# A hand-ordered prologue rewritten: halved dense units, four rotating PSUM banks, and the tail keys first on SyncE's queue

## Chip, core and metric

The kernel runs on one core of a Trainium2 chip. The metric is the device time of one execution in microseconds; the number given for the kernel before is the median of 13 runs.

## The reference

Two stages. The first is chunked attention for 4 batches, 8 heads, 768 positions and head size 64; every chunk of 32 positions sees 16 positions to its left, 8 to its right, and 8 memory rows. The second is a gated feed-forward layer on the 3072 x 512 result:

```python
for c in range(nc):
    k_full = np.concatenate([mem_k, k[:, :, l_start:r_end]], axis=2)
    v_full = np.concatenate([mem_v, v[:, :, l_start:r_end]], axis=2)
    scores = scale * np.matmul(q_c, k_full.transpose(0, 1, 3, 2))
    a = softmax(scores)
    out[:, :, c_start:c_end] = np.matmul(a, v_full)
x = out.transpose(0, 2, 1, 3).reshape(B * S, H * D)
gate = np.maximum(x @ w_gate, 0.0)
val = x @ w_val
return gate * val @ w_out
```

The softmax is written here as a call; the reference computes it with maximum, exponential and sum. The weights are 512 x 1536, 512 x 1536 and 1536 x 512.

## The kernel before

**Blocks, steps and units.** The 3072 rows are cut into 8 blocks of 384 rows, two to a batch. In each block the attention is done in four steps of 96 queries (three chunks at once, against a band of 120 keys and 8 memory rows, with a mask for what a chunk may not see). A step has scores (TensorE, L251, with the mask added by two matmuls at L245 where the step masks there), an exponential (ScalarE, L258), a mask by product (VectorE, L265, where it doesn't), values (TensorE, L269, with the sum in an extra column), a division (VectorE, L275 and L278) and a transposition of the result into `xT`.

The dense layer of a block has 12 units of 128 hidden columns. A unit multiplies `xT` by a column block of the gate weights (four matmuls of 384 columns, L299), takes the relu (ScalarE, L304), does the same with the value weights, and multiplies both (VectorE, L310) into `gvT`. Three output tiles (L329, L338) follow when all 12 units are there.

**The ordered prologue.** From block 2 on, loops set the order: the attention of a block lies between the dense units of the one before, its K and Q are turned by DMA transposes (L186, L191). Ahead of that, blocks 0 and 1 are written out by hand in the string `ORDER`. Every token is one piece of work: `ck01:D` casts the second half of K of block 0 on VectorE (D is VectorE, A ScalarE, P GpSimd), `key2` makes the key bands of a pair of heads by matmuls with a shifted unit matrix (L361), `key2e:A` evacuates them, `q01` and `kt0` turn Q and K on TensorE, `S3`, `x3`, `M3`, `P3`, `n3`, `T3`, `e3` are the parts of step 3 (steps 0 to 3 are of block 0, 4 to 7 of block 1), `G2` gathers V for a step (L394), `fg01`, `fr01`, `fv01`, `fm01` are gate, relu, value and product of unit 1 of block 0, `d3` is a warm-up of three small matmuls, and `wa`, `wA`, `wb`, `wc` load growing pieces of the gate and value weights. Each engine runs its own instructions in the order in which the tokens come.

The first four units of blocks 0 and 1 stand in `ORDER`. The units 4 to 11 of these blocks follow from a list `units`, with a table `hook` of what is done after which unit: at unit 0 and 1 ScalarE casts block 2's K and SyncE turns it, at 4 and 5 the same for Q, and the scores of block 2 begin at unit 13.

**PSUM.** Eight banks: 0 and 1 for the scores of even steps, 2 and 3 for the values, 4 and up for everything that `bank()` hands out in rotation. In the prologue the scores of odd steps use banks 6 and 7 (`self.sb`), so the rotation has two banks (`NG = [2]`); after the exponential of step 7 it has four.

**Loads.** SyncE issues the list `LOADS` in order: K and Q of block 0 in halves (`lk01`, `lk00`, `lq00`, `lq01`), V's extra rows (`lvx`), K of block 1, V of block 0 in halves, Q of block 1, and V of block 1 step by step. The extra keys of block 0 (8 memory rows, 8 tail rows, tile `kx`) come over ScalarE's and GpSimd's queues. GpSimd issues the weights. Its first weight load waits for Q of block 1, by a copy of one element:

```python
GATE = raw["q"][0:1, 1, 0, 0, 0:1]
            if nm == "wa":
                pl(gate, GATE)
```

In the same way the loads of block 2 on SyncE's queue, and the last weight loads, wait for the third pair of weight loads (`wc`):

```python
pl(raw["k"][0:1, 0, 0, 0, 0:1], w_gate_sb[0:1, 0, 1023:1024])
load_kq(2)
load_w(1024, 512)
```

Of the kernel before, what the change touches and what calls it, by code (L numbers as in the profile page):

```python
# [8 lines left out]
F16 = mybir.dt.float16  # L9

ALU = mybir.AluOpType
# [4 lines left out]
def kernel(  # L16
# [14 lines left out]
    B, H, S, D = q.shape  # L31
# [3 lines left out]
    QB = 96  # L35
# [4 lines left out]
    MB = 384  # L40
    NJ = MB // QB
    NT = MB // 128
    NBLK = B * S // MB
    NFC = DM // 128
    NDC = DFF // 128
    VW = D + 2
    R3 = 3
# [7 lines left out]
    xpool = ctx.enter_context(tc.tile_pool(name="xpool", bufs=4))  # L55
    xtpool = ctx.enter_context(tc.tile_pool(name="xtpool", bufs=2))
    gvpool = ctx.enter_context(tc.tile_pool(name="gvpool", bufs=2))
    grpool = ctx.enter_context(tc.tile_pool(name="grpool", bufs=3))
    opool = ctx.enter_context(tc.tile_pool(name="opool", bufs=6))
    pspool = ctx.enter_context(tc.tile_pool(name="pspool", bufs=1, space=bass.MemoryType.PSUM))  # L60
    ctx.enter_context(tc.manual_schedule())
# [1 line left out]
    PS = pspool.tile([128, 8, 512], F32, name="PS")  # L63
    rot = [0]

    NG = [2]

    def bank():
        n = 4 + rot[0] % NG[0]
        rot[0] += 1  # L70
        return n

    dve, act, pool, pe, sp = nc.vector, nc.scalar, nc.gpsimd, nc.tensor, nc.sync
# [9 lines left out]
    kx = wpool.tile([2 * NMEM, 2, H, D], F32, name="kx")  # L83
    vx = wpool.tile([2 * NMEM, H, D], F32, name="vx")
    kx16 = wpool.tile([128, H, D], F16, name="kx16")
    vx16 = wpool.tile([128, H, D], F16, name="vx16")
# [9 lines left out]
    ke = wpool.tile([128, R3, HP, NMEM], F16, name="ke")  # L96
# [3 lines left out]
    w_gate_sb = wpool.tile([128, NFC, DFF], F16, name="w_gate_sb")  # L100
    w_val_sb = wpool.tile([128, NFC, DFF], F16, name="w_val_sb")
# [22 lines left out]
    def turned_mask(name, product):  # L124
        d = (masks if product else negp)[name] = wpool.tile([128, QB], F16, name=f"{'mask' if product else 'negp'}_{name}")
        o = d.rearrange("p (t c) -> p t c", t=R3)
        i = neg[name].rearrange("p (c t) -> p t c", t=R3)
        if product:
            pool.tensor_scalar(out=o, in0=i, scalar1=-1.0, scalar2=None, op0=ALU.is_ge)  # L129
        else:  # L130
            pl(o, i)
# [14 lines left out]
    def rows(t, b, tok, parts):  # L146
        return bass.AP(tensor=t.tensor, offset=t[b, 0, tok, 0].offset, ap=[[D, parts], [S * D, H], [1, D]])

    def kx_rows(eng, b, d, t, mem, eng2=None):
        eng.dma_start(d[0:NMEM], mem[b].rearrange("h n d -> n h d"))  # L150
        (eng2 or eng).dma_start(d[NMEM:2 * NMEM], rows(t, b, MB, NMEM))
# [17 lines left out]
    def cast3(eng, c, n, a0=0, na=HP):  # L169
        i = n % 2  # L170
        d = (kn[:, i, 0:R3].rearrange("p t a c -> p a t c") if c == "k" else qn[:, i])[:, a0:a0 + na]
        eng(d.rearrange("p a t (x d) -> p a x t d", x=2),  # L172
            raw[c][:, i, 2 * a0:2 * a0 + 2 * na].rearrange("p (a x) t d -> p a x t d", x=2))
# [119 lines left out]

    gvT, xTs = {}, {}

    def dff_mm(n, w_sb, m):
        o = PS[:, bank(), 0:MB]
        for f in range(NFC):
            pe.matmul(o, lhsT=w_sb[:, f, 128 * m:128 * m + 128], rhs=xTs[n][:, f], start=(f == 0), stop=(f == NFC - 1))  # L299
        return o  # L300

    def relu(g_ps):
        g_relu = grpool.tile([128, MB], F16, name="g_relu")
        act.activation(g_relu, g_ps, ACT.Relu)  # L304
        return g_relu

    def product(n, m, vl_ps, g_relu):
        if n not in gvT:
            gvT[n] = gvpool.tile([128, NDC, MB], F16, name="gvT")
        dve.tensor_tensor(out=gvT[n][:, m].rearrange("p (t j c) -> p t j c", t=R3, j=NJ),  # L310
                          in0=vl_ps.rearrange("p (j t c) -> p t j c", t=R3, j=NJ),
                          in1=g_relu.rearrange("p (j t c) -> p t j c", t=R3, j=NJ), op=ALU.mult)

    def dff(n, m, mid=()):
        g = relu(dff_mm(n, w_gate_sb, m))
# [69 lines left out]
    def cast_v3(eng, h0=0, nh=H):  # L385
        eng(v16[:, h0:h0 + nh], vlong[:, 0, h0:h0 + nh])
# [11 lines left out]

    dve.memset(warm, 0.0)
    act.activation(warm, warm, ACT.Exp)  # L400
    kx_rows(act, 0, kx[:, 0], k, mem_k, pool)
    LOADS = "lk01 lk00 lq00 lq01 lvx lk1 lv01 lv00 lq1 lvm lv10 lv13 lv11 lv12".split()
    for tok in LOADS:
        c, r = tok[1], [int(ch) for ch in tok if ch.isdigit()]
        if tok == "lvx":
# [15 lines left out]
    def keep(n):  # L421
        for _ in range(n):
            pe.matmul(PS[:, 3, 4 * VW:512], lhsT=zero[:, 0:128], rhs=zero[:, 0:512 - 4 * VW], start=True, stop=True)
# [32 lines left out]
    for n in EARLY:  # L456
# [3 lines left out]

    ac = act.copy
    GATE = raw["q"][0:1, 1, 0, 0, 0:1]
    keep(20)
    st = [Step(0, j) for j in range(NJ)] + [Step(1, j) for j in range(NJ)]
    ORDER = """
        kx16:D ck01:D key2 ck00:D key3 key2e:A d3 key0 cq01:P key0e:A key3e:D key1 d3 q01 ke key1e:A cq00:P kee:A
        q01e:D q00 q00e:D ck11:P ck10:A vx16:D cv00:D d10 kt1 cv01:P S0 kt0 kt0e:D S1 kt1e:A x0:A b0:D G0 M0:D S2
        x1:A g0:A G1 P0 x2:A g1:A M1 G2 bm:D mlast:P bi0:D bi2:P wa:P cq11:D cq10:A n0:D q11 P1 S3 g2:A cv10:A M2:D
        q11e:D q10 n1:D x3:A G3 P2 q10e:D g3:A wA:P S4 x4:A M3 n2:D bi1:D T0 P3 e0:D T1 wb:P S5 T2 n3:D e1:D e2:D
        wc:P b3:P x5:A M4 P4 cv11:P T3 S6 S7 n4:D e3:A M5 cv13:P P5 n5:D T4 x6:A M6 fg00 x7:A e4:A cv12:P fr00:A  # L470
        M7:D fv00 P6 fg01 fv01 T5 n6:D fr01:A P7 e5:A fm00:D T6 e6:A fg03 fm01:D fg02 n7:D fr03:A T7 fr02:A e7:D
        fv03 fm03:D fv02 fg12 fr12:A fg10 fr10:A fg11 fm02:D fr11:A fv12 fg13 fv11 fv13 fr13:A fm12:D fv10 fm11:D
        fm13:D fm10:D
    """.split()
    dve_masks = [int(t[1]) for t in ORDER if t[0] == "M" and t.endswith(":D")]
    for i, s_ in enumerate(st):
        s_.pm = i not in dve_masks
    for m, i in {(s_.kd, s_.pm): 0 for s_ in st[:-1]}:
        turned_mask(m, not i)
    out_of = {}  # L480
    for tok in ORDER:
        nm, _, e = tok.partition(":")
        eng = {"D": dv, "A": ac, "P": pl, "": None}[e]
        c, r = nm[0], [int(ch) for ch in nm if ch.isdigit()]
        if c == "d":
            keep(r[0])
        elif nm == "kx16":
            eng(kx16[0:2 * NMEM], kx[:, 0])
        elif nm == "vx16":
            eng(vx16[0:2 * NMEM], vx)  # L490
        elif nm == "mlast":
            build_mask("last", NQB - 1)
            turned_mask("last", not st[-1].pm)
        elif nm[:2] in ("ck", "cq"):
            cast3(eng, nm[1], r[0], 2 * r[1], 2)
        elif nm[:2] == "cv":
            if r[0]:
                cast_v(eng, 1, r[1], 1)
            else:
                cast_v3(eng, 4 * r[1], 4)  # L500
        elif nm[:3] == "key":
            if e:
                eng(*out_of[nm[:-1]])
            else:
                out_of[nm] = keys(r[0])
        elif nm[:2] == "ke":
            if e:
                eng(*out_of["ke"])
            else:
                out_of["ke"] = key_ends()  # L510
        elif nm[:2] == "kt":
            if e:
                eng(*out_of[nm[:-1]])
            else:
                out_of[nm] = turn_k3(2 * r[0])
        elif c == "q":
            if e:
                eng(*out_of[nm[:-1]])
            else:
                out_of[nm] = turn_q3(r[0], 2 * r[1])  # L520
        elif nm[:2] == "bi":
            bands(1, eng, (r[0],))
        elif nm in ("b0", "b3", "bm"):
            bands(1, eng, ({"0": 3, "3": 4, "m": 5}[nm[1]],))
        elif c == "w":
# [3 lines that stand above are left out]
                load_w(0, 128)  # L529
            elif nm == "wA":  # L530
                load_w(128, 128)
            else:
                load_w(*{"b": (256, 256), "c": (512, 512)}[nm[1]])
        elif c == "S":
            st[r[0]].scores()
        elif c == "x":
            st[r[0]].soft()
            if r[0] == 7:
                NG[0] = 4
        elif c == "M":  # L540
            if e == "D":
                st[r[0]].mask()
        elif c == "G":
            out_of[nm] = gather_v(r[0])
        elif c == "g":
            eng(*out_of["G" + nm[1]])
        elif c == "P":
            st[r[0]].values()
        elif c == "n":
            st[r[0]].norm()  # L550
        elif c == "T":
            st[r[0]].turn_pe()
        elif c == "e":
            st[r[0]].turned(eng)
        elif nm[:2] in ("fg", "fv"):
            out_of[nm] = dff_mm(r[0], w_gate_sb if nm[1] == "g" else w_val_sb, r[1])
        elif nm[:2] == "fr":
            out_of[nm] = relu(out_of["fg" + nm[2:]])
        elif nm[:2] == "fm":
            product(r[0], r[1], out_of["fv" + nm[2:]], out_of["fr" + nm[2:]])  # L560
    for m in ("first", "int", "last"):
        if m not in masks:
            turned_mask(m, True)
# [131 lines left out]
```

## Time and profile before

| | |
|---|---|
| median of 13 runs | 238.79 us (236.4 to 242.15) |
| profiled execution | 237.12 us, span 235.4 us |
| TensorE busy | 225.0 us, 96% of the span |
| ScalarE, VectorE, GpSimd busy | 112.5, 108.3, 63.7 us |
| granted TensorE clock | 1.000 |
| moved by DMA | 38.63 MB, mean 164 GB/s |
| chain that ended last | TensorE 77%, DMA 17%, GpSimd 3% |

The span runs from the first to the last instruction; what lies around it makes up the rest of the execution's time. Busy time counts a matmul from its start to its modelled end, so it is not the share of the peak. A line number is that of the program before; after the change, lines below 398 keep theirs, and the later ones move down a little. In a timeline a row is the start, the duration, the engine and line, what is written and read, and in brackets how long the engine had stood idle and what released it.

### The profile page before, as it was taken

To read this page: it belongs to the slowest core of one execution; us is meant where nothing else is said; L and a number is where in the kernel's file an instruction comes from. 1 tells how busy PE (TensorE), PEld (TensorE's weight loads), DVE (VectorE), ACT (ScalarE), POOL (GpSimd) and SP (SyncE) were. 2 spreads that over 40 slices of the span, in tenths; PEclk is the share of its full clock that TensorE was granted. 3 is DMA by queue.
4 is the path that set the end of the run, shared out by engine and by line. 5 is a ranking of instruction groups with operands and counts; after the bars stand their busy time and mean duration, and the time that the engine had idled before them with its cause. 6 is when DMAs were issued, how large, how long until landed. Compare 5 with 4: busy or idle time off the path is not lost.

```text
span 235.4 us, 4758 instructions
## 1 busy us (share of the span) xinstructions
PE 225.0 (96%) x1817; PEld 135.5 (58%) x1817; DVE 108.3 (46%) x231; ACT 112.5 (48%) x201; POOL 63.7 (27%) x116
## 2 busy tenths in 40 slices
PE   6799899897999999999999999999999999999994
PEld 4656565454788755545554555555654556456543
DVE  3488743342640147604771277505770287314410
ACT  2386641753446356355653457344644455133312
POOL 7889320859550420005000510023000500000000
PEclk9999999999999999999999999999999999999999
DMA  6999999999999999389855997199846801220012
GB/s 184 318 260 190 202 218 213 152 173 236 224 184 185 254 266 211 58 198 249 218 124 116 236 288 149 36 224 290 179 95 152 134 1 36 77 90 0 4 45 91
DMA packets 91843, 38.63 MB, mean 164 GB/s; under 512 B 64260, under 2 KB 89604, under 8 KB 91820
## 3 DMA queue, kind: packets, MB, share of 16 engines
q1 hardware_dynamic: 73796, 32.52, 59.5%
q0 software_dynamic: 17952, 5.79, 22.8%
q8 instruction: 14, 0.23, 0.4%
q14 instruction: 9, 0.07, 0.1%
q10 hardware_dynamic: 72, 0.02, 0.0%
HBM read 30.24 MB, written 6.29 MB: 155 GB/s over the span
## 4 chain that ended last, share of the span: by engine, by line
PE 77%; DMA 17%; POOL 3%; SPq 1%; issue 0%; DVE 0%; ACT 0%; ACTq 0%; POOLq 0%
PE PS L299 45%; PE PS L329 19%; PE PS L338 8%; DMA kraw<-in_k_dram 6%; DMA qT<-qn 4%; DMA w_gate_sb<-in_moe_w_gate_dram 4%; DMA vraw<-in_v_dram 3%; PE PS L251 3%; PE PS L269 3%; POOL w_val_sb L449 1%; SPq L144 1%; POOL w_gate_sb L449 1%; POOL kb L208 0%; POOL gate L527 0%; POOL mask_last L129 0%
## 5 line engine op out<-in xcount | busy, mean ns | idle before, releaser
L310 DVE TENSOR_TENSOR gvT<-PS,g_relu 128x384 f16<-128x384 f32 x96 | 53.2, 555 | 90.2 <-PE PS L299 84.6
L299 PE MATMUL PS<-xT,w_gate_sb 128*128 128x384 f16 x384 | 77.8, 327 | 1.0 <-ACT g_relu L304 1.0
L299 PE MATMUL PS<-xT,w_val_sb 128*128 128x384 f16 x384 | 77.6, 326 | 0.5 <-ACT xT L290 0.5
L304 ACT ACTIVATE g_relu<-PS 128x384 f16<-128x384 f32 x96 | 47.1, 492 | 52.9 <-PE PS L299 32.5
L299 PEld LDWEIGHTS <-w_gate_sb 128*128 128x128 f16 x384 | 35.6, 98 | 25.0 <-issue 1.3
L299 PEld LDWEIGHTS <-w_val_sb 128*128 128x128 f16 x384 | 36.4, 98 | 23.4 <-issue 0.8
L329 PE MATMUL PS<-w_out_sb,gvT 128*128 128x512 f16 x204 | 45.8, 379 | 0.0
L208 POOL COPY kb<-kT 128x320 f16<-128x320 f16 (+1 forms) x19 | 14.8, 871 | 90.3 <-DMA kT<-kn 68.4
L329 PEld LDWEIGHTS <-gvT 128*128 128x128 f16 x204 | 19.6, 98 | 22.3
L258 ACT ACTIVATE ex<-PS 128x768 f16<-128x768 f32 x32 | 25.8, 812 | 9.4 <-PE PS L251 9.3
L332 ACT COPY o_sb<-PS 128x512 f32<-128x512 f32 x17 | 10.0, 586 | 34.0 <-PE PS L329 34.0
L278 DVE TENSOR_TENSOR x_big<-PS,rinv 96x512 f16<-96x512 f32 x32 | 22.0, 686 | 1.1
L338 PE MATMUL PS<-w_out_sb,gvT 128*128 128x256 f16 (+2 forms) x168 | 19.1, 272 | 0.0
L338 PEld LDWEIGHTS <-gvT 128*128 128x128 f16 x168 | 16.1, 98 | 2.4
L269 PEld LDWEIGHTS <-ex 128*128 128x128 f16 x256 | 12.0, 98 | 5.0 <-issue 0.7
L275 DVE RECIPROCAL rinv<-PS 96x8 f32<-96x8 f32 x32 | 6.5, 202 | 16.6 <-PE PS L269 16.3
L269 PE MATMUL PS<-vb,ex 128*128 128x66 f16 x256 | 13.4, 193 | 0.5 <-DVE x_big L278 0.5
L251 PEld LDWEIGHTS <-kb 64*128 64x128 f16 x256 | 6.4, 94 | 11.1 <-issue 10.7
L251 PE MATMUL PS<-qT,kb 64*128 64x96 f16 x256 | 10.8, 205 | 1.6 <-DMA qT<-qn 1.6
L172 ACT CAST kn<-kraw 128x768 f16<-128x768 f32 x13 | 10.7, 826 | 2.5 <-DMA kraw<-in_k_dram 2.5
L172 ACT CAST qn<-qraw 128x768 f16<-128x768 f32 x13 | 10.8, 833 | 0.9 <-DMA qraw<-in_q_dram 0.9
L341 ACT COPY o_sb<-PS 128x256 f32<-128x256 f32 (+2 forms) x14 | 5.2, 373 | 10.9 <-PE PS L338 10.4
(104 smaller groups left out, 129.6 us busy)
## 6 DMA issues: line engine op xcount, KB each, us to landing
kraw<-in_k_dram SPq DMA_DIRECT2D x7, 768.0 KB
qraw<-in_q_dram SPq DMA_DIRECT2D x7, 768.0 KB
vraw<-in_v_dram SPq DMA_DIRECT2D x20, 240.0 KB
out_dram<-o_sb SPq DMA_DIRECT2D x17, 256.0 KB
w_out_sb<-in_moe_w_out_dram POOLq DMA_DIRECT2D x6, 256.0 KB, 8.8
out_dram<-o_sb SPq DMA_DIRECT2D x12, 128.0 KB
w_gate_sb<-in_moe_w_gate_dram POOLq DMA_DIRECT2D x2, 512.0 KB, 9.6
w_val_sb<-in_moe_w_val_dram POOLq DMA_DIRECT2D x2, 512.0 KB, 12.0
```

The source lines that it names most:

```text
L172: eng(d.rearrange("p a t (x d) -> p a x t d", x=2), raw[c][:, i, 2 * a0:2 * a0 + 2 * na].rearrange("p (a x) t d -> p a x t d", x=2))
L208: eng(dst(1, r, [[128, nj], [R3, 40]]), src(kT, TS * t + P + (r > 0), [[PP, nj], [1, 40]]))
L251: pe.matmul(o.rearrange("p (t c) -> p t c", t=R3), lhsT=self.kb[r, a, j, :], rhs=qT_t[i][r, a, :, PP * j:PP * j + PP], start=not self.pm, ...
L258: act.activation(self.ex[:, :, 0:QB].rearrange("p (h b) c -> p b h c", b=2), PS[:, self.sb:self.sb + 2, 0:HP * QB].rearrange("p b (h c) -> ...
L269: pe.matmul(PS[:, 2 + h // 4, VW * (h % 4):VW * (h % 4) + VW], lhsT=self.ex[:, h, :], rhs=self.vb[:, self.j, h, :], start=True, stop=True)
L278: dve.tensor_tensor(out=self.x.rearrange("p (b h d) -> p b h d", b=2, h=4), in0=o[:, :, :, 0:D], in1=rb, op=ALU.mult)
L299: pe.matmul(o, lhsT=w_sb[:, f, 128 * m:128 * m + 128], rhs=xTs[n][:, f], start=(f == 0), stop=(f == NFC - 1))
L304: act.activation(g_relu, g_ps, ACT.Relu)
L310: dve.tensor_tensor(out=gvT[n][:, m].rearrange("p (t j c) -> p t j c", t=R3, j=NJ), in0=vl_ps.rearrange("p (j t c) -> p t j c", t=R3, j=NJ ...
L329: pe.matmul(PS[:, o], lhsT=gvT[n][:, m, 128 * t:128 * t + 128], rhs=w_out_sb[:, m, :], start=(m == 0), stop=(m == NDC - 1))
L332: act.copy(o_sb, PS[:, o])
L338: pe.matmul(o, lhsT=gvT[n][:, m, 128 * t:128 * t + 128], rhs=w_out_sb[:, m, c0:c1], start=(m == 0), stop=(m == NDC - 1))
```

## The change

It has several parts. The tail keys of block 0 go from GpSimd's queue to the head of SyncE's, and pieces in the load list change places. The order string is rewritten: tokens move, casts and evacuations change their engine, and masks change between VectorE and TensorE (one step, 6, is masked by product where it was three, 0, 2 and 7). The units 0 and 1 of both blocks are split into halves `a` and `b` of two steps (192 columns) each; `dff_mm`, `relu` and `product` get a range of columns. The rotation starts with four banks and goes to two at the first scores of an odd step. The relu tiles get five buffers in place of three.

```diff
-    grpool = ctx.enter_context(tc.tile_pool(name="grpool", bufs=3))
+    grpool = ctx.enter_context(tc.tile_pool(name="grpool", bufs=5))
...
-    NG = [2]
+    NG = [4]
...
-    def dff_mm(n, w_sb, m):
-        o = PS[:, bank(), 0:MB]
+    def dff_mm(n, w_sb, m, c0=0, w=MB):
+        o = PS[:, bank(), 0:w]
         for f in range(NFC):
-            pe.matmul(o, lhsT=w_sb[:, f, 128 * m:128 * m + 128], rhs=xTs[n][:, f], start=(f == 0), stop=(f == NFC - 1))
+            pe.matmul(o, lhsT=w_sb[:, f, 128 * m:128 * m + 128], rhs=xTs[n][:, f, c0:c0 + w], start=(f == 0), stop=(f == NFC - 1))
         return o
...
-    def product(n, m, vl_ps, g_relu):
+    def product(n, m, vl_ps, g_relu, j0=0, nj=NJ):
...
-        dve.tensor_tensor(out=gvT[n][:, m].rearrange("p (t j c) -> p t j c", t=R3, j=NJ),
-                          in0=vl_ps.rearrange("p (j t c) -> p t j c", t=R3, j=NJ),
-                          in1=g_relu.rearrange("p (j t c) -> p t j c", t=R3, j=NJ), op=ALU.mult)
+        dve.tensor_tensor(out=gvT[n][:, m].rearrange("p (t j c) -> p t j c", t=R3, j=NJ)[:, :, j0:j0 + nj],
+                          in0=vl_ps.rearrange("p (j t c) -> p t j c", t=R3, j=nj),
+                          in1=g_relu.rearrange("p (j t c) -> p t j c", t=R3, j=nj), op=ALU.mult)
...
-    kx_rows(act, 0, kx[:, 0], k, mem_k, pool)
-    LOADS = "lk01 lk00 lq00 lq01 lvx lk1 lv01 lv00 lq1 lvm lv10 lv13 lv11 lv12".split()
+    kx_rows(act, 0, kx[:, 0], k, mem_k, sp)
+    LOADS = "lk01 lk00 lq01 lq00 lvx lk1 lv00 lv01 lq1 lvm lv11 lv10 lv12 lv13".split()
...
-    keep(20)
+    keep(22)
...
-        kx16:D ck01:D key2 ck00:D key3 key2e:A d3 key0 cq01:P key0e:A key3e:D key1 d3 q01 ke key1e:A cq00:P kee:A
-        q01e:D q00 q00e:D ck11:P ck10:A vx16:D cv00:D d10 kt1 cv01:P S0 kt0 kt0e:D S1 kt1e:A x0:A b0:D G0 M0:D S2
-        x1:A g0:A G1 P0 x2:A g1:A M1 G2 bm:D mlast:P bi0:D bi2:P wa:P cq11:D cq10:A n0:D q11 P1 S3 g2:A cv10:A M2:D
-        q11e:D q10 n1:D x3:A G3 P2 q10e:D g3:A wA:P S4 x4:A M3 n2:D bi1:D T0 P3 e0:D T1 wb:P S5 T2 n3:D e1:D e2:D
-        wc:P b3:P x5:A M4 P4 cv11:P T3 S6 S7 n4:D e3:A M5 cv13:P P5 n5:D T4 x6:A M6 fg00 x7:A e4:A cv12:P fr00:A
-        M7:D fv00 P6 fg01 fv01 T5 n6:D fr01:A P7 e5:A fm00:D T6 e6:A fg03 fm01:D fg02 n7:D fr03:A T7 fr02:A e7:D
-        fv03 fm03:D fv02 fg12 fr12:A fg10 fr10:A fg11 fm02:D fr11:A fv12 fg13 fv11 fv13 fr13:A fm12:D fv10 fm11:D
-        fm13:D fm10:D
+        kx16:A ck01:D key3 ck00:D cq00:D key2 cq01:P mlast:P key0 key0e:D q01 key3e:A key2e:A q01e:A key1 q00
+        q00e:D ck10:P ck11:D key1e:A vx16:A ke d5 S1 d4 kt0 kt0e:D kt1 cv01:D kt1e:D x1:A S0 cv00:P wa:P S3 wA:P G0
+        x0:A kee:D b0:D M1 M0 bm:D x3:A G1 bi2:D g0:A g1:A cq11:D cq10:A P0 wb:P G2 bi0:D n0:D q11 S2 wc:P g2:D
+        q11e:A x2:A P1 q10 b3:P G3 M2 q10e:A g3:A cv11:P bi1:D n1:D P2 cv10:D T1 n2:D e1:A M3 S4 x4:A T0 e0:D M4 P3
+        S5 x5:A n3:D T2 S6 P4 x6:A T3 e3:A S7 x7:A e2:D n4:D fg01a M5 P5 fr01a:A fg01b M6:D fg00a cv12:P fr01b:A
+        fv01b fv00a M7 fr00a:A n5:D T4 fm01b:D P6 T5 e4:A fm00a:D n6:D fg00b cv13:P fv01a e5:A fv00b fm01a:D
+        fr00b:A fg11a fg10a P7 fm00b:D fr11a:A T6 fr10a:A n7:D fv10a fm10a:D fg03 fg02 e6:A T7 fv02 fr03:A fr02:A
+        e7:D fm02:D fv03 fg13 fg10b fr13:A fm03:D fg12 fv10b fr10b:A fv13 fm10b:D fm13:D fv12 fr12:A fg11b fv11a
+        fm12:D fm11a:D fr11b:A fv11b fm11b:D
...
         elif c == "S":
+            if r[0] % 2 and NG[0] == 4 and not two:
+                NG[0] = 2
+                two.append(1)
             st[r[0]].scores()
...
-        elif nm[:2] in ("fg", "fv"):
-            out_of[nm] = dff_mm(r[0], w_gate_sb if nm[1] == "g" else w_val_sb, r[1])
...
+        elif nm[:2] in ("fg", "fv", "fr", "fm"):
+            h = "ab".find(nm[4:]) if nm[4:] else -1
+            j0, nj = (0, NJ) if h < 0 else (h * NJ // 2, NJ // 2)
...
+                out_of[nm] = dff_mm(r[0], w_gate_sb if nm[1] == "g" else w_val_sb, r[1], QB * j0, QB * nj)
```

A mask token without an engine does nothing where it stands; the scores of that step carry the mask. The two mask products that no early step uses any more (first and last) are built on GpSimd after the ordered list, ahead of the copy that releases block 2's loads.

## The prediction

> **What bounds the kernel now.** I read the page first (slices, then the chain), then the chain of waits for the first 60 us, then TensorE's timeline, then the others and the windows. The page's second part says that TensorE is full almost everywhere:
>
> ```profile
> PE   6799899897999999999999999999999999999994
> DMA  6999999999999999389855997199846801220012
> ```
>
> A slice is 5.9 us. TensorE has gaps only in slices 0 to 9, that is, up to 59 us; the change touches the code that fills 0 to 38 us. So the question is what sets the end of that part. The chain of waits, cut to 0 to 60 us (start us, us, what), says that it isn't TensorE:
>
> ```profile
> 6.54 7.05 DMA vraw<-in_v_dram
> ...
> 15.35 1.10 POOL kb L208
> 16.45 0.74 POOL gate L527
> ...
> 21.19 8.83 DMA w_gate_sb<-in_moe_w_gate_dram
> 30.02 0.05 issue
> 30.07 0.19 POOL kraw L582
> 30.26 0.02 issue
> 30.28 10.66 DMA kraw<-in_k_dram
> ...
> 41.74 0.49 ACT g_relu L304
> ...
> 47.76 9.26 DMA qT<-qn
> 57.02 0.04 issue
> 57.06 0.35 PE PS L251 x8
> ```
>
> The chain runs through loads: block 0's V, the gate on GpSimd, the third pair of weight loads, the K of block 2 (which the copy at L582 holds back until those weights have landed), its cast on ScalarE, and the transposed Q of block 2, for which TensorE waits at the scores of unit 13. TensorE's timeline shows what that costs it, and what the start costs:
>
> ```profile
> 7.16 0.79 PE L361 MATMUL PS<-step,kn 128*128 128x360 f16 x6 [1.82 <-DVE kn L172]
> ...
> 42.28 0.81 PE L299 MATMUL PS<-xT,w_gate_sb 128*128 128x384 f16 x4 [1.05 <-ACT g_relu L304]
> ...
> 57.06 0.35 PE L251 MATMUL PS<-qT,kb 64*128 64x96 f16 x8 [1.63 <-DMA qT<-qn]
> ```
>
> The 1.05 us at 42.28 is ScalarE standing at the cast of block 2's K until 41.01. The 1.63 us at 57.06 is the transposed Q. After that no gap is listed up to the output tail. So between the end of the hand-ordered units (the last group starts at 36.5 and ends at 37.2) and 57.06 TensorE has 1.05 + 1.63 = **2.68 us of slack**: whatever the ordered part gains or loses above -2.68 us isn't seen at the end, as long as the loads arrive when they do now.
>
> **What the skill says, and whether the trace agrees.** (1) The Trainium skill, "DMA: Bandwidth & Descriptors", section "Queues, rings and completion order": each DMA engine takes turns, packet by packet, between the queues that have work. So weights issued earlier on GpSimd's queue take their share from SyncE's V loads and add no bandwidth by themselves. In the trace the windows give 182 GB/s for 15 to 18 us (nearly all SyncE's queue), 177 for 18 to 21 (both) and 205 for 21 to 30 (weights); the DMA share is above 1 in all three. That fits engines that never run dry. (2) The same page, "Anatomy of one DMA", puts about 2 us of fixed cost on a DMA, most of it receipt. Here the lag between the moment when the moved bytes add up and the landing is about 1 us: K's second piece adds up at 10.15 us and is seen at 11.2. (3) "TensorE: Matmul & The Clock Gate", section "Back-to-back issue gap": N/2.4 + 2.5 ns for a warm matmul, so two of 192 columns (165 ns) cost nearly one of 384 (162.5). The trace's groups of four 384-column matmuls stand 0.65 us apart, which is 162 ns each; no 192-column row exists yet.
>
> **The change, part by part.**
>
> *Tail keys first on SyncE's queue.* One DMA leaves GpSimd (0.71 us at 1.44) and stands ahead of all of SyncE's loads. Its issue rows on SyncE are 0.28 us (L151 at 3.44) and 0.38 (L151 at 31.23). All of K, Q and V of blocks 0 and 1 move that much later: I take **+0.3 us** (ends 0.2 and 0.5). The halves that change places in the load list have equal sizes, so whole tensors land no later for it. For the compute it is a gain: VectorE now waits for those keys until 6.22,
>
> ```profile
> 6.22 0.41 DVE L488 CAST kx<-kx 16x512 f16<-16x512 f32 x1 [3.22 <-DMA kx<-in_k_dram]
> ```
>
> and casts K's first half only after that, though the chain has it landed at 4.66. After: landed 4.66 + 0.3 = 4.96, cast 0.54, first keys at about 5.6 instead of 7.16. The 22 warm-up matmuls (20 took 4.05 us, so about 4.4) end at 5.7. So TensorE starts the keys some **1.4 us** earlier.
>
> *The new order up to the values.* The gathers need both halves of block 0's V, the later of which landed at 13.59 and now at 13.9; cast 0.57, so the second part of the first gather goes from 14.24 to about 14.5. By then TensorE has also done one more set of scores (0.28 + 0.33 of mask). From there 22.9 us of TensorE time lie before the last unit's end now (14.24 to 37.1, 1.03 of it listed idle). Same work less 0.6, from 14.5: 35.8 without stalls, 36.8 with as much idle as now. Bounds: 35.8 and 39 (the first gate half now needs the second pair of weight loads, issued at 18.27 and 19.01, landing a median 5.5 us later, 23.8 and 24.5; TensorE gets there at about 23.3).
>
> *Masks.* Two more steps take the mask on TensorE: 4 matmuls x 162 ns = 0.65 us more there, 2 x 0.55 us less on VectorE, inside the slack. On GpSimd two products (L129) move behind the last V casts, before the copy that releases block 2's K. They cost 0.44 to 1.56 us each; GpSimd ends its list at 25.78 now and then waits 4.29 us for weights, so they are hidden, unless that list ends more than 4.2 us later.
>
> *Halves.* Four pairs of units are split: 32 more matmuls, no more columns, so about 0.1 us. Four relus of 0.49 us become eight; the nearest smaller row is the 256-column copy at 0.37, so +0.7 to +1.0 on ScalarE. Four products of 0.56 become eight of 0.28 to 0.56: +0 to +2.2 on VectorE, I take 0.6. From 21 to 30 us VectorE is busy 7.27 of 9 us and ScalarE 5.74, so there is room, and what doesn't fit falls under the same 2.68.
>
> *Four banks before the first odd scores, five relu buffers.* They take waits away from evacuations before 11 us, where the list waits for loads anyway: nothing.
>
> *GpSimd's way to the weights.* This is the one part that touches the chain. Casts of Q (0.83) and the band copy L208 (1.10) leave GpSimd ahead of the gate. The gate then waits for block 1's Q. The bytes up to it (4.0 MB) add up at 15.0 us in the 1-us windows; with 1 us of lag it lands at 16.0, after the change at 16.3. The gate's end goes from 17.19 to between 16.5 (L582, a like copy, takes 0.18) and 17.2 (this copy took 0.84), so the weights are issued **0 to 0.7 us earlier**. But does the third gate load land earlier? After block 1's Q, 1.05 MB of V and 1.57 MB of weights precede its last byte, 2.62 MB; the windows moved 3x182 + 3x177 + 8x205 = 2.72 MB from 15 to 29 us, and it landed at 30.02. The engines are full, so an earlier issue only reorders. Weights joining 0.6 us earlier at 205 instead of 182 GB/s give 14 KB, 0.07 us. The landing thus follows the start of SyncE's queue: +0.3 - 0.1 = **+0.2 us** (ends: -0.7, if it follows the issue; +0.5).
>
> **Sum.** TensorE's gain of about 1 us turns into a longer wait at unit 3 (1.05 becomes about 2.3). Block 2's K, its transposes and the scores at 57.06 move with the weights, +0.2. The profiled execution was 237.12 us (span 235.4 and 1.7 around it); it would be 237.3. The median of the 13 runs is 238.79, 1.67 above that execution; I put the same difference on it: **239.0**.
>
> **Rivals.** *Earlier weights pay (faster).* If the DMA engines weren't full between 15 and 21 us, the third pair lands with its issue: 0.7 earlier, and 0.3 more because the row that took 1.05 us at 21.19 takes the 0.75 of its neighbours. That is -1.0 (237.8), and with block 2's K meeting less of the last value load up to the whole 2.68: 236.1. If the median execution, 1.67 us above the profiled one, is longer because of TensorE's start, the 1 to 1.4 us gained there also show: 237.4. For it: 177 to 182 GB/s, against 205 later and 326 at 12 us. Against: DMA shares of 1.2 and 1.4. I give it 0.30, about 237.3.
>
> *The head of SyncE's queue (slower).* The tail keys are 64 runs of 256 bytes. The same DMA took 4.7 us to land from GpSimd in an empty machine. If the bulk behind it starts with that latency and not with the issue time, everything on SyncE's queue, the gate and the weights slip by 1.2 to 1.8 us, and the end with them: 240.3. It decides from a slip of 1.2 us; the sign is DMA traffic of under 150 GB/s at 3 to 4 us, where it is 364 now. Against: vx's two such DMAs hold the queue for 0.73 us at 2.96 and the traffic stays at 293 and more. 0.26.
>
> *TensorE becomes the bound.* The ordered part would have to end 2.68 us later, at about 39.8, beyond my bound. A few per cent, in the slower case.
>
> *The change does nothing measurable* is the forecast: 0.44.
>
> **Range.** Two in ten left out: 237.0 to 240.7; for the likeliest case alone 237.7 to 239.9. Differences under about 0.5% (1.2 us) can't be told from none in this kernel.
>
> **What would show it.** Right: first keys at about 5.6 us; weights issued at 16.5 to 17.2; the copy that releases block 2's K at 30.0 to 30.5; the wait at unit 3 above 2 us; the scores of unit 13 still ended by the transposed Q at 57.0 to 57.5. Wrong: that copy before 29.2 or after 31.2, or no wait left at unit 3.

## The result, and the profile after

The changed kernel takes 241.05 us (median of 11 runs, 239.45 to 242.05), the kernel before 239.42 (48 runs, 235.18 to 243.45). The ratio is **1.0144, 95% interval 1.0108 to 1.0180**: slower, by less than 2%. The medians are 0.7% apart; the ratios here compare, of each kernel, the executions within 1.5% of its fastest, which are all of the changed kernel's and 19 of the 48 of the kernel before, so both numbers are given where they say different things.

The profiled execution of the changed kernel took 239.57 us, span 237.9. Its page has TensorE's slices and its granted clock (slices are counted from 0 and are 5.9 us long). The dip has moved to slices 3 and 4 (18 to 30 us), and in slices 4 and 5 (24 to 36 us) the clock isn't full:

```profile
PE   7985899999999999999999999999999999999994
...
PEclk9999679999999999999999999999999999999999
```

Two numberings of the units meet below. "Unit 4" is a number of hidden columns, as in `ORDER`: it is the first unit behind the ordered part, and its start marks the end of that part. "Unit 3" and "unit 13", where TensorE waits, and the units of the `hook` table are places in the list `units`, counted from 0 at that first unit.

TensorE's timeline before the change has step 4's scores in one row and unit 4 here:

```profile
20.88 0.34 PE L251 MATMUL PS<-qT,kb 64*128 64x96 f16 x8
...
37.16 0.81 PE L299 MATMUL PS<-xT,w_gate_sb 128*128 128x384 f16 x4
```

After the change, the rows that answer to those and to those of the prediction:

```profile
5.68 0.79 PE L361 MATMUL PS<-step,kn 128*128 128x360 f16 x6
...
21.03 0.22 PE L251 MATMUL PS<-qT,kb 64*128 64x96 f16 x2
23.96 0.30 PE L251 MATMUL PS<-qT,kb 64*128 64x96 f16 x6 [2.72 <-POOL kb L218]
...
28.92 0.80 PE L299 MATMUL PS<-xT,w_gate_sb 128*128 128x192 f16 x4 [0.96 <-ACT ex L258]
...
42.59 0.81 PE L299 MATMUL PS<-xT,w_gate_sb 128*128 128x384 f16 x4
...
59.59 0.34 PE L251 MATMUL PS<-qT,kb 64*128 64x96 f16 x8
```

The keys start at 5.68 as forecast (7.16 before). But in the middle of step 4's scores, after two of eight matmuls, TensorE stands still for 2.72 us until GpSimd has made a band copy, L218. The row at 42.59 is unit 4; before it was 37.16. The waits at unit 3 and at unit 13 (59.59) are gone: TensorE is now later than the loads. Windows of 4 us from 20 to 36 us; the columns are the window, its length, then busy time and count of TensorE, weight loads, VectorE, ScalarE and GpSimd, the granted clock, the DMA share and GB/s:

```profile
20.00:24.00 4.00, 1.28 (x20) 0.73 (x20) 1.43 (x4) 1.31 (x3) 4.00 (x7) 1.00 1.67 180
24.00:28.00 4.00, 3.96 (x62) 2.54 (x63) 2.81 (x7) 2.71 (x4) 2.88 (x6) 0.72 1.37 205
28.00:32.00 4.00, 3.08 (x25) 2.88 (x25) 0.89 (x2) 1.80 (x4) 1.75 (x3) 0.50 1.13 181
32.00:36.00 4.00, 4.00 (x60) 3.81 (x59) 2.94 (x8) 2.28 (x6) 0.00 (x0) 0.93 1.08 253
```

After the standstill the granted clock is a half from 25.8 to 32.6 us (read in windows of 0.1 us), and TensorE counts as busy while it does less. The chain of waits names what stood ahead of the band copy:

```profile
16.53 0.57 POOL gate L528
17.10 0.94 POOL w_gate_sb L449
...
22.52 0.74 POOL w_val_sb L449
23.26 0.66 POOL kb L218
23.92 0.05 issue
23.96 0.30 PE PS L251 x6
...
37.20 22.45 PE PS L299 x148
59.65 0.28 PE PS L251 x8
```

The chain goes from the gate (Q of block 1) through eight weight issues to the copy, then along TensorE alone. The copy is token `b3`: it makes the keys of step 7. It stands behind the weights on GpSimd in both kernels, and ran at nearly the same time in the kernel before:

```profile
22.99 0.65 POOL L218 COPY kb<-kT 128x480 f16<-128x480 f16 x1
```

Before, its token came after the scores of the steps 4 and 5, which so didn't wait for it; after, it comes ahead of step 4's. Step 4 reads other columns of the same tile. Its first two matmuls (head pair 0) didn't wait and the six of pairs 1 to 3 did, which fits a dependency tracker that takes the copy's strided target (one step's columns of all four head pairs) as one interval from its first to its last address. That is inferred from the pattern and not shown; that step 4 doesn't need the copy is shown by the first experiment.

The theory to test is that this misplaced token makes the loss, by the wait and by the half clock after it, and that the rest of the change brings nothing that is seen. The rivals are that the halves, masks and banks cost the time, or that the wait alone does.

### The profile page after: what moved, and what is told of

Same layout as the page of the kernel before. It is cut to its first block, busy times and chain, and to the rows that moved or that the text cites. A ratio compares the mean times of both kernels' runs of the same rounds, so it can differ in the third digit from the quotient of the medians.

```text
span 237.9 us, 4842 instructions
## 1 busy us (share of the span) xinstructions
PE 228.5 (96%) x1857; PEld 140.5 (59%) x1857; DVE 108.9 (46%) x234; ACT 114.5 (48%) x206; POOL 61.5 (26%) x115
## 4 chain that ended last, share of the span: by engine, by line
PE 88%; DMA 5%; POOL 3%; SPq 1%; ACT 0%; issue 0%; ACTq 0%
PE PS L299 54%; PE PS L329 19%; PE PS L338 8%; DMA qraw<-in_q_dram 3%; PE PS L269 3%; PE PS L251 3%; DMA kraw<-in_k_dram 2%; POOL w_gate_sb L449 1%; SPq L144 1%; POOL w_val_sb L449 1%; PE PS L287 1%; PE PS L245 0%; ACT ex L258 0%; POOL kb L218 0%; POOL gate L528 0%
## 5 line engine op out<-in xcount | busy, mean ns | idle before, releaser
L310 DVE TENSOR_TENSOR gvT<-PS,g_relu 128x384 f16<-128x384 f32 (+1 forms) x100 | 53.9, 539 | 87.4 <-PE PS L299 87.2
L299 PE MATMUL PS<-xT,w_gate_sb 128*128 128x384 f16 (+1 forms) x400 | 79.2, 324 | 1.0 <-ACT ex L258 1.0
L299 PE MATMUL PS<-xT,w_val_sb 128*128 128x384 f16 (+1 forms) x400 | 78.4, 322 | 0.0
L304 ACT ACTIVATE g_relu<-PS 128x384 f16<-128x384 f32 (+1 forms) x100 | 47.7, 478 | 55.8 <-PE PS L299 39.0
L299 PEld LDWEIGHTS <-w_gate_sb 128*128 128x128 f16 x400 | 37.4, 99 | 24.1 <-issue 0.9
L299 PEld LDWEIGHTS <-w_val_sb 128*128 128x128 f16 x400 | 38.0, 99 | 21.7
L208 POOL COPY kb<-kT 128x480 f16<-128x480 f16 (+1 forms) x18 | 13.7, 854 | 96.1 <-DMA kT<-kn 74.2
L258 ACT ACTIVATE ex<-PS 128x768 f16<-128x768 f32 x32 | 25.8, 812 | 12.6 <-PE PS L251 12.6
L338 PEld LDWEIGHTS <-gvT 128*128 128x128 f16 x168 | 16.1, 98 | 2.4
L251 PE MATMUL PS<-qT,kb 64*128 64x96 f16 x256 | 11.4, 208 | 2.7 <-POOL kb L218 2.7
L265 DVE TENSOR_TENSOR ex<-ex,mask_int 128x768 f16<-128x768 f16 x19 | 10.6, 557 | 0.0
```

The costliest lines, as they stand in the source:

```text
L208: eng(dst(1, r, [[128, nj], [R3, 40]]), src(kT, TS * t + P + (r > 0), [[PP, nj], [1, 40]]))
L251: pe.matmul(o.rearrange("p (t c) -> p t c", t=R3), lhsT=self.kb[r, a, j, :], rhs=qT_t[i][r, a, :, PP * j:PP * j + PP], start=not self.pm, ...
L258: act.activation(self.ex[:, :, 0:QB].rearrange("p (h b) c -> p b h c", b=2), PS[:, self.sb:self.sb + 2, 0:HP * QB].rearrange("p b (h c) -> ...
L265: dve.tensor_tensor(out=e, in0=e, in1=m8, op=ALU.mult)
L338: pe.matmul(o, lhsT=gvT[n][:, m, 128 * t:128 * t + 128], rhs=w_out_sb[:, m, c0:c1], start=(m == 0), stop=(m == NDC - 1))
```

## The experiments

**1. The copy just ahead of its user** (and the V cast behind it on GpSimd).

```diff
-        ... q10 b3:P G3 M2 q10e:A g3:A cv11:P bi1:D ... T3 e3:A S7
+        ... q10 G3 M2 q10e:A g3:A bi1:D ... T3 e3:A b3:P cv11:P S7
```

> The changed kernel with the band copy of step 7 (L218, token b3) moved in the order string from ahead of step 4's scores to just ahead of step 7's; on GpSimd it still follows all eight weight issues. Theory (step 4 waits for a copy that it doesn't need, and the half TensorE clock that follows the standstill makes the loss large): no wait of over 0.5 us before step 4's scores, clock 1.0 throughout, the ordered part ends at 37 to 38.5 us instead of 43.2, and the time is that of the kernel before, ratio 0.993 to 1.004. Rival A (the halves, the masks on TensorE and the two banks cost the time): the wait goes, but the ratio stays above 1.010. Rival B (the wait only moves to step 7, which does need the copy): 1 us or more of idle there, and a ratio of 1.005 to 1.014.

Measured: ratio 1.0012 (0.9970 to 1.0054), median 239.38 against 238.71. TensorE's timeline:

```profile
21.61 0.34 PE L251 MATMUL PS<-qT,kb 64*128 64x96 f16 x8
...
25.92 0.49 PE L299 MATMUL PS<-xT,w_gate_sb 128*128 128x192 f16 x4 [1.03 <-ACT ex L258]
...
37.86 0.81 PE L299 MATMUL PS<-xT,w_gate_sb 128*128 128x384 f16 x4
...
56.74 0.35 PE L251 MATMUL PS<-qT,kb 64*128 64x96 f16 x8 [1.81 <-DMA qT<-qn]
```

All eight matmuls of step 4 run together, the clock is 1.0, unit 4 starts at 37.86 instead of 42.59, and unit 13 waits for the transposed Q as it did before the change. Both rivals of this run fall: the loss isn't there without the wait, and no wait of 1 us appears at step 7.

**2. Warm-ups in the standstill**, 27 of them ahead of step 4's scores, the wait left as it is.

```diff
-        ... M3 S4 x4:A T0
+        ... M3 d9 d9 d9 S4 x4:A T0
```

> The changed kernel with 27 warm-up matmuls ([...]2.8 us) ahead of step 4's scores, in the time in which TensorE stands still; the wait itself stays. Theory: step 4's scores still go on at 24.0 us, but the clock stays at 1.0, the half-clock stretch from 25.9 to 32.7 us is gone with about 3.3 us of TensorE time, the ordered part ends at 39.5 to 40 us, which is inside the 2.68 us of slack, and the ratio is 0.998 to 1.006. Rival (the wait alone makes the loss, the clock is incidental): ratio above 1.009.

Measured: 1.0157 (1.0098 to 1.0217), 6 runs, 239.32 to 244.29 us.

```profile
22.39 3.02 PE L423 MATMUL PS<-zero 128*128 128x248 f16 x27 [0.84 <-DVE x_big L278]
...
25.67 0.34 PE L251 MATMUL PS<-qT,kb 64*128 64x96 f16 x8
...
41.84 0.81 PE L299 MATMUL PS<-xT,w_gate_sb 128*128 128x384 f16 x4
```

The clock is 1.0, but the expectation fails. The warm-ups could start only behind a division of VectorE (0.84 us), step 4's scores began 0.6 us after the copy was done (25.67 against 25.08), and in this execution the gate came 0.96 us later than in the profile above. Unit 4 started at 41.84, 2 us later than expected. The clock was 0.999 or 1.0 in five of the six executions, and these took 239.32 to 242.14 us, as long as those of the changed kernel: with the clock kept, the time isn't won back.

**3. The kernel before, with that token early.** Its weight tokens go with it, in the same order on GpSimd.

```diff
-        ... g3:A wA:P S4 ... T1 wb:P S5 ... wc:P b3:P x5:A
+        ... g3:A wA:P wb:P wc:P b3:P S4 ... T1 S5 ... x5:A
```

> The kernel before with nothing changed but the place of that one token: the band copy of step 7 (and the weight tokens ahead of it on GpSimd, whose order there stays) moved ahead of step 4's scores. Theory: step 4's scores wait for it until about 23.7 us (2.5 us), the clock halves, the ordered part ends 5 us later, 2.68 of that is slack, and the ratio is 1.008 to 1.016, the whole loss of the change. Rival (the loss comes from other parts of the change): ratio 1.000 to 1.004.

Measured: 1.0062 (1.0031 to 1.0093). The trace shows the same fault:

```profile
21.79 0.22 PE L251 MATMUL PS<-qT,kb 64*128 64x96 f16 x2
24.84 0.42 PE L251 MATMUL PS<-qT,kb 64*128 64x96 f16 x6 [2.83 <-POOL kb L218]
...
42.61 0.81 PE L299 MATMUL PS<-xT,w_gate_sb 128*128 128x384 f16 x4
```

Two matmuls, a wait of 2.83, the clock at 0.50 from 24 to 28 us and 0.65 to 32, unit 4 at 42.61. So the token alone makes a loss in the kernel before, but less than half of the 1.44%, below what was expected; the medians don't show it (238.43 and 238.71). From gate to unit 4 the token costs 4.4 us here (42.61 - 17.53 = 25.1, where the kernel before has 37.16 - 16.45 = 20.7) and 5.2 us in the changed kernel (42.59 - 16.53 = 26.1, where experiment 1 has 37.86 - 17.00 = 20.9). These are single executions, the one shown here the longest of its 14 (240.86 us). The 0.8 us between the two costs would be some 0.3% of the time; the rest of the difference is open.

**4. The copy ahead of the weights**, in GpSimd's idle time before the gate.

```diff
-        ... S0 cv00:P wa:P S3 wA:P G0 ... bm:D x3:A ... q10 b3:P G3
+        ... S0 cv00:P S3 G0 ... bm:D b3:P wa:P wA:P x3:A ... q10 G3
```

> The changed kernel with the band copy moved into GpSimd's idle time ahead of the gate (13.5 to 16.5 us there), before the weight issues. Theory: it runs at about 15.6 us, nobody waits for it, the ordered part ends at 36 to 38 us, TensorE waits 1.5 to 3 us at unit 3 for block 2's K, and the ratio is 0.992 to 1.002, the forecast on record. Rival (other parts cost): above 1.008.

Measured: 1.0026 (0.9973 to 1.0079), median 239.46 against 238.71. The ratio is just above the expected 1.002, its interval covers 1 and lies below that of the change (from 1.0108). The loss is gone by a second road. The profile is of the longest of the 22 executions (244.16 us):

```profile
22.58 0.34 PE L251 MATMUL PS<-qT,kb 64*128 64x96 f16 x8
...
38.87 0.81 PE L299 MATMUL PS<-xT,w_gate_sb 128*128 128x384 f16 x4
...
62.85 0.50 PE L251 MATMUL PS<-qT,kb 64*128 64x96 f16 x8 [6.03 <-POOL kb L225]
```

Step 4's scores run together and the ordered part isn't held up. What makes this execution long lies behind it: the transpose of block 2's K took 14.8 us, and TensorE stood 6.03 us at unit 13.

**5. Fewer warm-ups**, 18 in place of 27.

> The changed kernel with 18 warm-up matmuls (1.9 us) in place of 27 ahead of step 4's scores. With 27, the block began 0.84 us late, behind the division of step 2, and ended 0.6 us after the copy was there. If the half clock is a part of the loss: clock 1.0, the ordered part ends at the release of step 4's scores plus 16.2 us (in the changed kernel it was 23.96 to 42.6, 18.6 us), so some 2.4 to 3 us earlier for the same release, and the ratio falls to 1.000 to 1.009. If the clock is incidental: ratio 1.010 to 1.018 as with the change itself.

Measured: 1.0193 (1.0127 to 1.0259), 6 runs. The trace and the time part ways:

```profile
22.52 2.06 PE L423 MATMUL PS<-zero 128*128 128x248 f16 x18 [0.84 <-DVE x_big L278]
...
25.25 0.30 PE L251 MATMUL PS<-qT,kb 64*128 64x96 f16 x6 [0.18 <-POOL kb L218]
...
41.37 0.81 PE L299 MATMUL PS<-xT,w_gate_sb 128*128 128x384 f16 x4
...
59.04 0.34 PE L251 MATMUL PS<-qT,kb 64*128 64x96 f16 x8 [0.60 <-POOL kb L225]
```

From the release to unit 4 it takes 41.37 - 25.25 = 16.1 us, against 42.59 - 23.96 = 18.6 with the half clock: the half clock costs 2.5 us of the ordered part, as expected. The time didn't fall: five executions at a clock of 1.0 took 239.01 to 241.26 us. The gate was at 17.62, 1.1 us later than in the changed kernel's profile, and block 2's K took 10.6 us to be transposed (its chain: cast, 44.79 to 55.35, bands to 59.0). With six runs in each of the experiments 2 and 5 the clock's share of the *time* stays open.

**6. Block 2's loads released by the second pair of weight loads**, in the kernel before.

```diff
-    pl(raw["k"][0:1, 0, 0, 0, 0:1], w_gate_sb[0:1, 0, 1023:1024])
+    pl(raw["k"][0:1, 0, 0, 0, 0:1], w_gate_sb[0:1, 0, 511:512])
```

> The kernel before with one edit: block 2's K and Q (and the last weight loads) are released by the second pair of weight loads, not the third. If the chain of loads bounds the kernel before (2.68 us of TensorE waiting at units 3 and 13): both waits go or shrink below 0.5 us together, and the ratio is 0.986 to 0.994. If those waits come back elsewhere (the third pair of weights now late for unit 4, at 37 us): ratio 0.996 to 1.005.

Measured: ratio 0.9992 (0.9953 to 1.0032), but 235.25 to 237.66 with a median of 236.08 against 238.53 (234.75 to 243.08). The wait at unit 13 didn't go (1.70 us). What went are the long executions.

**7. The same release with the copy moved** (experiments 1 and 6 together).

> The changed kernel with the band copy just ahead of step 7 (as in the first experiment) and block 2's K and Q released by the second pair of weight loads. If the change's earlier TensorE start was real and only hidden behind the loads: the ordered part ends at about 37 us with no wait at units 3 and 13, and the ratio is 0.982 to 0.992, at or below that of the kernel before with the same release. If the rest of the change brings nothing: the same ratio as that one within 0.003.

Measured: 1.0132 (1.0053 to 1.0211), 6 runs. Unit 4 started at 37.36, so the ordered part was in time, but unit 13 waited 2.42 us for Q, and after that wait the clock was a half: the first 16 dense matmuls took 4.39 us. First the wait (timeline) and these matmuls (chain) here, then the same of experiment 6:

```profile
57.41 0.35 PE L251 MATMUL PS<-qT,kb 64*128 64x96 f16 x8 [2.42 <-DMA qT<-qn]
57.75 4.39 PE PS L299 x16
```

```profile
56.62 0.35 PE L251 MATMUL PS<-qT,kb 64*128 64x96 f16 x8 [1.70 <-DMA qT<-qn]
56.97 2.71 PE PS L299 x16
```

The spans of these two executions differ by 2.4 us (237.4 and 235.0): 0.8 of it is the later start of unit 13, 1.7 the half clock. Here, where no wait for loads follows, the half clock is paid in full. Of the six executions, five have a clock of 0.993 and took 238.79 to 241.02 us; the one with 1.0 took 236.95. Neither expectation holds. The second one, that the rest of the change brings nothing, asked for the ratio of experiment 6 within 0.003; it is 0.014 above it, and the medians are 3.45 us apart.

**8. A delay of 3 us**, TensorE busy, ahead of unit 4 in the kernel before.

```diff
-        fm13:D fm10:D
+        fm13:D fm10:D d9 d9 d9 d2
```

> The kernel before with 29 warm-up matmuls (3.0 us, TensorE stays busy) after the last hand-ordered product, ahead of unit 4. It measures the slack by itself. As on record (slack 2.68 us at the scores of unit 13): those scores at 57.1 to 57.5 us, ratio 1.000 to 1.003. If the slack ends earlier, because ScalarE casts block 2's K and Q only after the units 0, 1, 4 and 5, so that 3.0 us late units make casts and transposes 1.9 us later: scores of unit 13 at 58.5 to 59.5, ratio 1.004 to 1.012.

Measured: 1.0103 (1.0071 to 1.0135): 2.4 of 3.0 us are seen. Unit 4, the transpose of Q on SyncE, and unit 13, from two timelines:

```profile
41.26 0.81 PE L299 MATMUL PS<-xT,w_gate_sb 128*128 128x384 f16 x4
...
61.48 0.35 PE L251 MATMUL PS<-qT,kb 64*128 64x96 f16 x8 [3.16 <-DMA qT<-qn]
```

```profile
45.71 3.83 SPq L186 DMA_TRANSPOSE kT<-kn  x1
49.84 4.90 SPq L191 DMA_TRANSPOSE qT<-qn  x1
```

Q's transpose is issued at 49.84 instead of 47.76, since ScalarE casts Q after the relus of the units 4 and 5 of the list; and it took 11.6 us in place of 9.26. This profile is of one of the longest of the 23 executions (243.19 us), so it shows how the delay is passed on, not how large its cost is. Medians are equal (238.57 and 238.41), the lowest runs 2.9 us apart (237.70 and 234.81). So the slack is large in long executions and nearly absent in short ones.

**9 and 10. All of the chain eased**, in the kernel before and in the changed kernel with the copy of experiment 1: early release, the last weights issued at unit 0, Q's casts and transpose at the units 2 and 3.

```diff
-    load_kq(2)
-    load_w(1024, 512)
+    load_kq(2)
...
-        0: [lambda: cast_kx(pl, 1), lambda: cast3(ac, "k", 2, 0, 2)],
+        0: [lambda: cast_kx(pl, 1), lambda: load_w(1024, 512), lambda: cast3(ac, "k", 2, 0, 2)],
```

> The kernel before with the load chain eased: block 2's K and Q are released by the second pair of weight loads, the last weight loads are issued at unit 0 instead of together with K, and Q's casts and transpose go from units 4 and 5 to units 2 and 3. If that chain bounds the kernel before: no wait of TensorE over 0.5 us from unit 0 to unit 13, a span of 232.5 to 233.5 us, a narrow spread, median 1 to 2% below that of the kernel before. If the transposes or the late weights take the bound again: a wait of 1 us or more at unit 8 or 13 and less than 0.5%.

> The changed kernel with its band copy just ahead of step 7, and the same three edits on block 2's loads. If the rest of the change starts the dense units earlier, but hidden behind the loads: 0.3 to 1.2 us below the kernel before with the same edits. If the rest brings nothing: within 0.5 us of it.

Measured: 1.0086 (1.0051 to 1.0121) and 1.0178 (1.0118 to 1.0239). Both are worse, and the second by 0.9% more than the first, with medians of 242.62 and 239.29 us. The chain of the first:

```profile
40.72 12.65 DMA kT<-kn
...
57.05 0.50 PE PS L251 x6
57.55 4.13 PE PS L299 x16
```

K's transpose starts 2.3 us earlier and takes 12.65 us instead of 8.0, now beside the last weights; that they slow it is likely and not shown. Unit 13 waits 2.69 us, and the clock falls to a half. In the second it waits for Q:

```profile
60.34 0.50 PE L251 MATMUL PS<-qT,kb 64*128 64x96 f16 x8 [4.02 <-DMA qT<-qn]
```

**11. The copy ahead of the third weight pair only.**

```diff
-        ... P0 wb:P G2 ... q10 b3:P G3
+        ... P0 wb:P b3:P G2 ... q10 G3
```

> The changed kernel with the band copy moved two places on GpSimd, ahead of the third pair of weight issues (1.5 us). Step 4's scores still wait for it, but 1.0 to 1.4 us instead of 2.7. If the standstill has to be long to halve the clock: clock 1.0, the ordered part ends 16 to 16.4 us after the release (18.6 with the half clock), at about 38.7 us for a gate at 16.5, and most of the loss is gone, ratio 1.002 to 1.007. If the loss is proportional to the wait: ratio 1.006 to 1.009 with a drop of the clock.

Measured: 1.0060 (1.0008 to 1.0113), median 239.02 against 238.79.

```profile
24.05 0.30 PE L251 MATMUL PS<-qT,kb 64*128 64x96 f16 x6 [1.61 <-POOL kb L218]
...
40.17 0.81 PE L299 MATMUL PS<-xT,w_gate_sb 128*128 128x384 f16 x4
...
60.62 0.35 PE L251 MATMUL PS<-qT,kb 64*128 64x96 f16 x8 [3.38 <-DMA qT<-qn]
```

A wait of 1.61 us leaves the clock at 1.0 through the ordered part and the release to unit 4 at 16.1 us, as expected; the ratio lies between 1 and that of the change. The profile is of one of the longer executions (242.23 us): at unit 13 TensorE stood 3.38 us, and there the clock did fall to a half, for 3.4 us.

**12. Experiment 6 again.**

> The kernel before with block 2's loads released by the second pair of weights, once more, on other executions: the first had a median 1.0% below the kernel before, a spread of 2.4 us in place of 8, and a ratio of the fast runs of 0.9992. If it only cuts the slow executions: the median again 0.6 to 1.2% below, the lowest again at 235.0 to 235.5, not below the kernel before's lowest. If the first was chance: median within 0.3%.

Measured: median 235.95 (22 runs, 235.46 to 240.18) against 238.79 (43 runs, 234.74 to 243.32), 1.2% below; ratio 0.9986 (0.9959 to 1.0014). By its median it beats both kernels, by cutting the long executions; its shortest ones are no shorter.

## Why the prediction was wrong, step by step

- **Keys at 5.6 us**: right (5.68). **Second part of the first gather at 14.5**: it began at 15.02, half a microsecond off.
- **The end of the ordered part, 35.8 to 39 us: this step failed.** It was 42.6. The forecast took GpSimd's tokens for what they do to the weights and never asked who waits for L218, so this wait and the clock after it stood at nothing in its sum. What the runs show in their place is 2.7 us of wait (step 4's six matmuls begin at 23.96; without it they would have followed the first two at 21.03 + 0.22 = 21.25) and 2.5 us of half clock (18.6 instead of 16.1 us from release to unit 4). Experiments 1 and 4 take the wait away and with it the loss; 1 puts the end at 37.86, inside the bounds.
- **Slack of 2.68 us: this step failed too, as a property of the kernel.** Between the two profiled executions it holds: unit 4 is 5.4 us later and unit 13 2.5. But it was read from one execution, 2 us above the shortest of the kernel before, and it took the end of the waits as fixed by the loads, where K's and Q's casts are paced by the units themselves. In experiment 8 a delay of 3.0 us is seen with 2.4 (0.0103 of 236.3 us), where 2.68 us of slack would let through 0.3.
- **Weights issued 0 to 0.7 us earlier, landing +0.2**: the gate ended at 17.10 (17.19 before), the copy that releases block 2's K ran at 29.92 (30.07). The landing was 0.15 us earlier and not later, within the ends that were given, and without weight for the result.
- **Halves**: after the change eight matmuls of 192 columns take 0.66 us (33.49 to 34.15), 82 ns each, as taken; a relu half took 0.33 us (0.37 taken), a product half 0.36 (0.35 taken). **Masks on GpSimd**: 0.51 and 0.49 us, hidden, as worked out.
- **The rivals.** The slower case was named for the head of SyncE's queue; the queue slipped by 0.4 us (K's first half landed at 5.05 instead of 4.66), and the mechanism didn't happen. The end came from the one that got a few per cent, TensorE as the bound. Its sign, no wait left at unit 3, was named as a sign of being wrong, and it came.
- **The rest of the change brings nothing**: this part of the forecast stands with the loads as they are, as far as intervals of half a per cent go (1.0012 and 1.0026). It doesn't stand once block 2's loads are released early: there the rest of the change costs, 1.0132 against 0.9992 and 1.0178 against 1.0086. In the profiles unit 13 waits longer there (2.42 us against 1.70, 4.02 against 2.69); which part of the change brings that wasn't tried.
- **The number**: the median lies 2.05 us above the forecast of 239.0. Of this, 0.63 is the kernel before, whose median is 239.42 over 48 runs where the forecast started from 238.79.

Open are how much of the time, not of the trace, belongs to the half clock in the ordered part (experiments 2 and 5 keep the clock and gain nothing measurable), why the token alone costs 0.6% in the kernel before and 1.4% here, and what each of the halves, masks and banks does by itself.

## What to carry to other kernels

When an order is rewritten, go through every producer that now stands ahead of a reader of the same tile, and ask when its engine gets to it: a dependency that nobody needs costs as much as a real one when the producer is queued behind a batch of DMA issues. A stall that is read off one profile is slack only in executions like that one; put a delay in to measure it. And a wait of TensorE is dearer than its length when the clock drops after it: in experiment 7 a wait of 2.42 us was followed by 1.7 us of lost time.

## What the runs showed of the hardware

- In these profiles the granted TensorE clock fell to a half in or after every standstill of TensorE of 2.13 us and more (2.13, 2.42, 2.69, 2.72, 2.83, 3.16, 3.38, 4.02 and 6.03 us), and after none of up to 1.82 us. The place of the 1.82 us in the prediction, the first keys, shows both sides. In experiment 8 the wait there was 2.13 us and the clock from 8 to 12 us 0.57:

```profile
7.38 0.79 PE L361 MATMUL PS<-step,kn 128*128 128x360 f16 x6 [2.13 <-DVE kn L172]
```

```profile
8.00:12.00 4.00, 4.00 (x32) 2.71 (x31) 0.69 (x1) 1.17 (x2) 2.61 (x5) 0.57 1.10 314
```

- The half clock lasted 3.4 us (after 2.13, 2.42, 2.69, 3.16, 3.38 and 4.02 us) or 6.8 us (after 2.72, 2.83 and 6.03 us), so its length doesn't follow that of the standstill. It began 2.0 to 4.5 us after TensorE had stopped: at the earliest 4.0 us before work went on, at the latest 1.8 us after, in the changed kernel. The Trainium skill, "TensorE: Matmul & The Clock Gate", section "What's actually happening", gives one idle window of about 3.4 us as the condition; here less was enough.
- The mean clock of an execution counts these stretches: one of 3.4 us at half clock takes 0.007 from the mean over 238 us (an estimate from these two numbers). None of the changed kernel's twelve executions is without: two have 0.992 or 0.993 (239.45 and 239.58 us), five 0.984 or 0.985 (239.57 to 241.37), five 0.977 or 0.978 (241.05 to 242.05). Between the first two groups the times hardly differ. Of 159 executions of the kernel before that were measured beside the experiments, 73 have 0.998 or more (median 237.44 us), 51 about 0.99 (238.80) and 35 0.986 or less (241.48). This goes together with the time; it doesn't say which makes which.
- A DMA transpose of the same K block (SBUF to SBUF, 16 tiles) landed 8.0 us after its issue in the kernel before, and 10.6, 11.0, 12.7 and 14.8 us after it in the experiments 5, 3, 9 and 4. The gate on block 1's Q began between 16.5 and 18.4 us. Much of the spread of this kernel's executions may hang on these two, which single profiles can't show.
